# First tiles and first block issued from strings of single operations in a new order

## The chip, the cores and the metric

One core of a Trainium2 chip runs the kernel. TensorE (PE, with its weight loads PEld), VectorE (DVE), ScalarE (ACT) and GpSimd (POOL) each work through their own queue in order; SyncE (SP) issues the DMAs. The metric is the device time of one execution in microseconds; profiles give times from the start of their span.

## The reference

Attention within chunks of 64 tokens, then two matrix products with an ELU between. q, k and v are float32, the weights float64.

```python
scores = scale * np.matmul(q_c, k_c.transpose(0, 1, 2, 4, 3))   # 8 x 8 heads, 9 chunks of 64, head size 64
scores = scores - np.max(scores, axis=-1, keepdims=True)
attn = np.exp(scores)
attn = attn / (np.sum(attn, axis=-1, keepdims=True) + 1e-09)
out = np.matmul(attn, v_c)
...
h = x @ w_in                                                    # 4608 x 512 by 512 x 2048
g = np.where(h > 0.0, h, alpha * (np.exp(np.minimum(h, 0.0)) - 1.0))
return (g @ w_out).astype(np.float32)
```

## The kernel before

The 4608 tokens are nine blocks of 512, a block four tiles of 128 tokens; the hidden size of 2048 is sixteen tiles f of 128. Each operand of a product is held as a high and a low part (xhi, xlo; wi_hi, wi_lo; ghi, glo; wo_hi, wo_lo), and a product is three matmuls (`three`, L419): high by high, high by low, low by high. So the hidden product of one f (`hidden`, L428) is 4 x 3 matmuls into a bank h, and the second product of one f (`second_products`, L867, through a queue) 4 x 3 matmuls into the banks o of the four tiles. Between them stands `elu` (L436): relu and exp on ACT, one operation on DVE (e), ghi on ACT, glo on DVE. On PE the order is h0, h1, o0, h2, o1 and so on, one f apart.

The weights are 64-bit floats. They come in seventeen units: unit u holds the slice u of w_in (stored as `moe_w_in`) and the slice u - 1 of w_out. A unit takes two conversions on ACT (`prepare_units`, L128: "high" at L135, "low" at L140), three steps on DVE (L164, L171, L177), behind the third a copy of each high part on ACT (L184, wi_hi and wo_hi), and a subtraction of each low part on DVE (L155, wi_lo and wo_lo). Three staging buffers (`st`) take turns, and a unit's load is issued when the third step of the unit two earlier is done.

`early_attention` (L265) handles a tile in ten steps: transposes of q and k on PE (L271), their copies qT and kT on ACT (L278), scores (L249), maximum and subtraction on DVE (L284, L300), exponential on ACT (L304), sums and scaling on DVE (L306 to L309), turning on PE (L316), a copy on ACT (L323), the product with v (L257), and the splitting into xhi on ACT and xlo on DVE (L413, L414). Tiles named in `BY_HEAD` take eight exponentials of one head each, which also give the sums (L294), in place of one exponential and DVE's subtraction and sum.

The program has no scheduler for PE, ACT, DVE and SP: each engine's queue is the order in which the code is written. The first four tiles follow the string `START` (a digit advances that tile by a step, r is a conversion, d a DVE step or subtraction of a unit, w a number of transposes of the identity matrix). The first block follows `FIRST_BLOCK`, four lines that serve all four groups of four f alike: H is `hidden`, e a step of `elu`, a a step of the group's early tile (tiles 4 to 7, which belong to the second block), P the second products of the f before, X the splitting of the second block's x into xhi and xlo (`split_next`, L847). Ahead of H the program makes sure that the unit of that f is split (`split_upto`). `LOADS` gives the order of the first DMAs. Before h0 ten transposes of the identity are issued. POOL is scheduled by itself; its first work is at the end of the first block (`combine`, L476).

Of the kernel before, what the change touches and what calls it, by code (L numbers as in the profile page):

```python
# [10 lines left out]
F32 = mybir.dt.float32  # L11
# [9 lines left out]
def kernel(  # L21
# [19 lines left out]
    nc = tc.nc  # L41
# [104 lines left out]
    def split_units():  # L146
# [6 lines left out]
        def subtract(u: int):  # L153
            for (hi, lo), w in before:
                nc.vector.tensor_tensor(out=lo, in0=w, in1=hi.bitcast(F32), op=ALU.subtract)  # L155
                yield
            split.append(u)

        before = []
        for u in range(NU):  # L160
# [14 lines left out]
            if u > 2:  # L175
                yield from subtract(u - 1)
# [3 lines left out]
            if PRELOADED <= u + 2 < NU:  # L180
                load_unit(u + 2)
            before = [(part, y[:, i].bitcast(F32)) for i, part in enumerate(parts)]
            for (hi, _), w in before:
                nc.scalar.copy(out=hi, in_=w)  # L184
# [6 lines left out]
    split = []  # L191
    splitting = split_units()

    def split_upto(u: int):
        while u not in split:
            next(splitting)
# [68 lines left out]
    def early_attention(tt: int, q_sb, k_sb, v_sb, kT, at, a_pool, pool, put, by_head: bool):  # L265


        both = pool.tile([P, 2, DM], F32, name="ps_a")
# [57 lines left out]
        multiply_v(x_ps, v_sb, aT.rearrange("p h (u t) -> p u h t", u=2))  # L326
# [392 lines left out]
    def warm(n: int):  # L719

        warm_ps = ps_start.tile([P, 2, DM], F32, name="ps_a")[:, 0, :].rearrange(
            "p (i t) -> p i t", i=4)
        for i in range(n):
            nc.tensor.transpose(out=warm_ps[:, i % 4, :], in_=ident, identity=ident)  # L724
# [3 lines left out]
    LOADS = "q0 k0 q1 k1 q2 k2 u0 q3 k3 v0 v1 u1 v2 v3"  # L728
    BY_HEAD = (3,)
    START = (  # L730
        "w13 0 1 0 1 0 0 1 0 2 2 2 1 3 0 r 0 1 1 3 3 1 r 0 0 2 3 2 d 1 3 d d 2 r 3 1 2 d 3 d 2 0 "
        "3 2 1 2 3 w10 3 r d d d d r r d"
    )
    FIRST_BLOCK = (
# [64 lines left out]
    PRELOADED = sum(item[0] == "u" for item in LOADS.split())  # L799
# [10 lines left out]
    with (  # L810
# [4 lines left out]
        loaded = {}  # L815
        for item in LOADS.split():
            kind, n = item[0], int(item[1:])
            if kind == "u":
                load_unit(n)
            else:  # L820
                loaded[item] = load_heads(
                    {"q": q, "k": k, "v": v}[kind], f"{kind}_sb", n * P, start)
        tiles = [early_attention(
            tt, *[loaded[f"{kind}{tt}"] for kind in "qkv"],
            start.tile([P, NK, P], F32, name="kT"), start, start, ps_start, split_first_x,
            tt in BY_HEAD,
        ) for tt in range(NTT)]
        for item in START.split():
            if item[0] == "w":
                warm(int(item[1:]))  # L830
            else:
                next({"d": splitting, "r": preparation}.get(item) or tiles[int(item)])
# [5 lines left out]
    wi1 = plain.enter_context(tc.tile_pool(name="wi1", bufs=1))  # L838
    weights.append((*w_in_tiles(wi1), *later_w_out))
    io = plain.enter_context(tc.tile_pool(name="io", bufs=2))  # L840
    ps_h = ctx.enter_context(tc.tile_pool(name="ps_h", bufs=2, space=bass.MemoryType.PSUM))
    ps_o = ctx.enter_context(tc.tile_pool(name="ps_o", bufs=1, space=bass.MemoryType.PSUM))
    early = ctx.enter_context(ExitStack())
    ps_early = early.enter_context(
        tc.tile_pool(name="ps_early", bufs=1, space=bass.MemoryType.PSUM))
# [7 lines left out]
    def early_tile(n: int):  # L853

        n0 = n * P
        loaded = [load_heads(src, name, n0, pool)
                  for src, name, pool in ((q, "q_sb", io), (k, "k_sb", io), (v, "v_sb", vio))]
        return early_attention(
            n % NTT, *loaded, k_turned, at, wi1, ps_early, lambda tt, src: keep_x(tt, src), True)
# [14 lines left out]
    following = early_tile(NTT)  # L874
    for blk in range(PLAIN - 1):
        if blk == 1:
            early.close()
            ps_a = ctx.enter_context(
                tc.tile_pool(name="ps_a", bufs=1, space=bass.MemoryType.PSUM))
        run = blk * TB, o_tiles(), None  # L880
        for f in range(NF):
            tt, st = divmod(f, 4)
            n = (blk + 1) * NTT + tt + 1
            if st == 0:
# [160 lines left out]
```

## Time and profile before

| | us |
|---|---|
| median of 3 runs (845.35 to 848.22) | 846.59 |
| the profiled execution | 848.72 |
| its span | 846.7 |
| first matmul of h0 | 26.74 |
| first matmul of o0 | 38.47 |
| first matmul of the second block's first hidden product | 133.32 |

Rows of the timeline and of the chain of waits begin with start and duration in us, then engine, line of the kernel, operation and tiles; what stands in brackets is the idle time of that engine just before and what ended it. Rows of the windows give the stretch, its length, the busy time of each engine with the number of its instructions, the granted clock of TensorE as a share of full speed, the busy share of the DMA engines (over 1 where transfers overlap) and GB/s.

### The profile page before, as it was taken

What the parts mean: (1) busy time and instruction counts of PE and PEld (TensorE: products, weight loads), DVE (VectorE), ACT (ScalarE), POOL (GpSimd) and SP (SyncE); (2) the same over time, 40 slices, a digit from 0 to 9 for tenths busy, and PEclk for the clock granted to TensorE, in tenths of its full rate; (3) what the DMA queues carried; (4) which work ended last, traced back from release to release, by engine and by line L of the source; (5) the groups of instructions that cost most, each with busy time, mean ns of one, the idle gap of its engine ahead of it and who ended that gap; (6) DMA issues with size and microseconds to landing.
All of it is one profiled execution on the core that took longest, in us unless ns stands there. A gap on an engine that the chain in (4) does not pass through costs nothing.

```text
span 846.7 us, 15737 instructions
## 1 busy us (share of the span) xinstructions
PE 829.1 (98%) x5959; PEld 678.1 (80%) x5959; DVE 501.2 (59%) x717; ACT 483.7 (57%) x855; POOL 176.5 (21%) x148
## 2 busy tenths in 40 slices
PE   6899999999999999999999999999999999999998
PEld 5687887888878887888888888788888888888786
DVE  5888996666775769666666745666555333233411
ACT  6799985544564547656656436556664355555521
POOL 0000005355302120211113531111126211111120
PEclk9799999999999999999999999999999999999999
DMA  9877672767768786698887656798854365545231
GB/s 240 259 214 228 220 223 75 223 201 240 240 191 229 207 220 183 185 252 247 236 257 243 183 151 208 197 257 242 225 159 137 109 195 162 164 142 161 92 108 50
DMA packets 178795, 164.10 MB, mean 194 GB/s; under 512 B 65568, under 2 KB 161312, under 8 KB 178720
## 3 DMA queue, kind: packets, MB, share of 16 engines
q1 hardware_dynamic: 178720, 163.10, 66.0%
q8 instruction: 47, 0.77, 0.4%
q14 instruction: 28, 0.23, 0.1%
HBM read 131.07 MB, written 28.31 MB: 188 GB/s over the span
## 4 chain that ended last, share of the span: by engine, by line
PE 90%; ACT 3%; DMA 2%; DVE 2%; SPq 1%; issue 1%; DVEq 0%; ACTq 0%
PE o L422 44%; PE h L422 41%; PE ps_a L249 2%; PE ps_a L257 2%; SPq L213 1%; DMA k_sb<-in_k_dram 1%; PE ps_a L316 1%; DMA v_sb<-in_v_dram 1%; DMA wi_hi<-a_dram 1%; DMA turned<-unturned 0%; DVE g_kept L590 0%; PE ps_a L271 0%; ACT e L440 0%; ACT e L587 0%; DVE xlo L850 0%
## 5 line engine op out<-in xcount | busy, mean ns | idle before, releaser
L422 PE MATMUL o<-wo_hi,ghi 128*128 128x512 f32 x416 | 165.4, 398 | 0.0
L422 PE MATMUL o<-wo_hi,glo 128*128 128x512 f32 x416 | 163.1, 392 | 0.2 <-DMA wi_hi<-a_dram 0.2
L422 PE MATMUL o<-wo_lo,ghi 128*128 128x512 f32 x416 | 162.8, 391 | 0.0
L597 POOL TENSOR_TENSOR glo<-e,ghi 128x512 fp32r<-128x512 f32 x46 | 59.6, 1296 | 317.3 <-ACT ghi L595 311.8
L422 PE MATMUL h<-xhi,wi_hi 128*128 128x512 f32 x336 | 112.1, 392 | 0.1
L422 PE MATMUL h<-xlo,wi_hi 128*128 128x512 f32 x336 | 111.4, 390 | 0.7 <-DVE xlo L850 0.7
L422 PE MATMUL o<-wo_hi,wo_lo 128*128 128x512 f32 x320 | 99.8, 390 | 1.0 <-DVE kept L455 1.0
L422 PEld LDWEIGHTS o<-wo_hi,ghi 128*128 128x128 f32 x416 | 78.6, 189 | 17.4 <-ACT ghi L447 0.2
L422 PEld LDWEIGHTS o<-wo_hi,glo 128*128 128x128 f32 x416 | 78.5, 189 | 17.5 <-DVE glo L450 1.0
L422 PEld LDWEIGHTS o<-wo_lo,ghi 128*128 128x128 f32 x416 | 78.6, 189 | 15.8
L636 ACT COPY kept<-h 128x512 f32<-128x512 f32 x72 | 42.3, 588 | 61.6 <-PE h L422 61.6
L422 PE MATMUL h<-wi_lo,wi_hi 128*128 128x512 f32 x288 | 75.0, 396 | 0.0
L422 PE MATMUL h<-xhi,wi_lo 128*128 128x512 f32 x192 | 74.9, 390 | 0.0
L422 PEld LDWEIGHTS h<-xlo,wi_hi 128*128 128x128 f32 x336 | 63.1, 188 | 14.0 <-DVE xlo L850 1.1
L422 PEld LDWEIGHTS h<-xhi,wi_hi 128*128 128x128 f32 x336 | 63.1, 188 | 13.6 <-PE ps_a L724 0.3
L422 PE MATMUL h<-wo_lo,wi_hi 128*128 128x512 f32 x288 | 73.0, 389 | 0.0
L422 PEld LDWEIGHTS o<-wo_hi,wo_lo 128*128 128x128 f32 x320 | 60.1, 188 | 14.4 <-DVE kept L455 1.9
L590 DVE SCALAR_TENSOR_TENSOR g_kept<-e,g_kept 128x512 f32<-128x512 f32 x48 | 35.5, 739 | 57.7 <-ACT e L587 57.7
L640 DVE TENSOR_TENSOR g_kept<-h,kept 128x512 f32<-128x512 f32 x48 | 33.1, 689 | 51.7 <-ACT kept L636 27.2
L422 PEld LDWEIGHTS h<-wo_lo,wi_hi 128*128 128x128 f32 x288 | 54.1, 188 | 11.2
L587 ACT ACTIVATE e<-e 128x512 f32<-128x512 f32 x96 | 60.7, 633 | 3.1
L422 PE MATMUL o<-wo_lo 128*128 128x512 f32 x160 | 62.3, 389 | 0.0
(107 smaller groups left out, 1318.0 us busy)
## 6 DMA issues: line engine op xcount, KB each, us to landing
wi_hi<-a_dram SPq DMA_DIRECT2D x168, 256.0 KB, 3.9
wo_lo<-lo_dram SPq DMA_DIRECT2D x52, 512.0 KB, 4.7
kept<-in_q_dram SPq DMA_DIRECT2D x100, 128.0 KB, 3.4
kept<-in_k_dram SPq DMA_DIRECT2D x100, 128.0 KB, 3.8
st<-in_moe_w_in_dram SPq DMA_DIRECT2D x16, 512.0 KB, 4.9
v_sb<-in_v_dram SPq DMA_DIRECT2D x32, 256.0 KB, 5.8
st<-in_moe_w_out_dram SPq DMA_DIRECT2D x16, 512.0 KB, 5.3
a_dram<-kept SPq DMA_DIRECT2D x16, 512.0 KB, 4.0
```

The costliest lines, as they stand in the source:

```text
L213: nc.sync.dma_start(out=dst[p0:p0 + n], in_=src[b, :, s0:s0 + n, :].rearrange("h s d -> s h d"))
L249: nc.tensor.matmul(scores[halves[c], j, hp, :], lhsT=qT[halves[j], hp, halves[c]], rhs=kT[halves[j], hp, halves[c]], start=True, stop=True,)
L257: nc.tensor.matmul(x_ps[halves[j], c, hp, :], lhsT=v_sb[halves[c], 2 * hp + j, :], rhs=aT[halves[c], :, j * NK + hp], start=True, stop=True,)
L316: nc.tensor.matmul(turned_ps[half, h, :], lhsT=a[half, h, :], rhs=ident[half, half], start=True, stop=True,)
L422: nc.tensor.matmul(ps, lhsT=a, rhs=b, start=start, stop=stop, skip_group_check=onto)
L587: nc.scalar.activation(out=e, in_=e, func=AF.Exp, scale=-1.0)
L590: nc.vector.scalar_tensor_tensor(out=to, in0=e, scalar=-1.0, in1=c, op0=ALU.add, op1=ALU.max)
L597: engine.tensor_tensor(out=lo, in0=e, in1=hi.bitcast(F32), op=ALU.subtract)
L636: nc.scalar.copy(out=c21 if i == 4 else self.kept[i - 1], in_=x_ps)
L640: nc.vector.tensor_tensor(out=to, in0=y_ps, in1=self.kept[kept], op=ALU.add)
```

## The change

`LOADS` goes; the loads stand in `START` now, with q, k and v of the four tiles ahead of unit 0, and unit 2 among them. `FIRST_BLOCK` becomes one string of single operations for all sixteen f: besides H, e, P, X a digit advances that tile, L begins a tile's loads, u loads a unit, r is a conversion, d a DVE step of a unit, s one subtraction of a low part (now apart from the steps, `subtract_next`), l writes a low part of w_out to memory, K begins the loads for tile 8. `split_upto` goes, and the order of the strings alone holds. The ten transposes before h0 go. `hidden` of f = 0, in each of the three blocks that use it, takes the eight matmuls with xhi first and the four with xlo last. Tile 2 in place of tile 3, and tiles 4 and 5 but not 6 and 7, are handled by head (before, tiles 4 to 7 all were). Pools whose memory was used by the first tiles wait for single tiles of it (`reuse_waits`). Behind X a copy of one element on POOL reads the last xlo and writes where one of POOL's additions writes later.

```diff
-        def subtract(u: int):
-            for (hi, lo), w in before:
-                nc.vector.tensor_tensor(out=lo, in0=w, in1=hi.bitcast(F32), op=ALU.subtract)
-                yield
-            split.append(u)
-
-        before = []
...
-            if u > 2:
-                yield from subtract(u - 1)
             nc.vector.scalar_tensor_tensor(
                 out=y, in0=high, scalar=0x80000000, in1=y, op0=ALU.bitwise_and, op1=ALU.bitwise_or
             )
-            if PRELOADED <= u + 2 < NU:
-                load_unit(u + 2)
-            before = [(part, y[:, i].bitcast(F32)) for i, part in enumerate(parts)]
-            for (hi, _), w in before:
-                nc.scalar.copy(out=hi, in_=w)
-            yield
-            if u <= 1:
-                yield from subtract(u)
-        yield from subtract(NU - 1)
+            for i, (hi, _) in enumerate(parts):
+                nc.scalar.copy(out=hi, in_=y[:, i].bitcast(F32))
+                merged.append((parts[i], y[:, i].bitcast(F32)))
+            yield
+
+    def subtract_next():
+        (hi, lo), w = merged.pop(0)
+        nc.vector.tensor_tensor(out=lo, in0=w, in1=hi.bitcast(F32), op=ALU.subtract)
...
-    def early_attention(tt: int, q_sb, k_sb, v_sb, kT, at, a_pool, pool, put, by_head: bool):
-
-
-        both = pool.tile([P, 2, DM], F32, name="ps_a")
+    def early_attention(tt: int, q_sb, k_sb, get_v, kT, at, a_pool, get_banks, put, by_head: bool):
+
+
+        both = get_banks()
...
-        multiply_v(x_ps, v_sb, aT.rearrange("p h (u t) -> p u h t", u=2))
+        multiply_v(x_ps, get_v(), aT.rearrange("p h (u t) -> p u h t", u=2))
...
-        for kt in range(NK):
-            three(h, hi[:, kt, :], lo[:, kt, :], xhi[:, kt, :], xlo[:, kt, :],
-                  kt == 0, kt == NK - 1)
+        if f:
+            for kt in range(NK):
+                three(h, hi[:, kt, :], lo[:, kt, :], xhi[:, kt, :], xlo[:, kt, :],
+                      kt == 0, kt == NK - 1)
+        else:
+            terms = [(w, xhi, kt) for w in (hi, lo) for kt in range(NK)]
+            terms += [(hi, xlo, kt) for kt in range(NK)]
+            for i, (w, x, kt) in enumerate(terms):
+                nc.tensor.matmul(h, lhsT=w[:, kt, :], rhs=x[:, kt, :], start=i == 0,
+                                 stop=i == len(terms) - 1)
...
-    LOADS = "q0 k0 q1 k1 q2 k2 u0 q3 k3 v0 v1 u1 v2 v3"
-    BY_HEAD = (3,)
+    BY_HEAD = (2, 4, 5)
...
-        "w13 0 1 0 1 0 0 1 0 2 2 2 1 3 0 r 0 1 1 3 3 1 r 0 0 2 3 2 d 1 3 d d 2 r 3 1 2 d 3 d 2 0 "
...
+        "q0 k0 q1 k1 w13 v0 0 1 0 q2 0 k2 q3 0 k3 1 1 v1 0 2 v2 1 3 0 2 2 v3 1 2 3 u0 3 1 2 u1 0 "
+        "r r 1 3 1 0 3 2 2 d u2 d 1 0 r d 3 3 2 s 2 0 r d 1 d 3 r 2 3 3"
...
-        "r H e d e a r e a d d e P",
...
+        "H r u3 r d L4 d e s 4 d 4 e e s r d e u4 H d s 4 e s r P e 4 d e e H 4 e d 4 L5 e s u5 d "
...
+        def start_step(item: str):
+            tt = int(item)
+            if tt not in tiles:
+                tiles[tt] = early_attention(
+                    tt, *[loaded[kind, tt] for kind in "qk"], lambda: loaded["v", tt],
+                    start.tile([P, NK, P], F32, name="kT"), start, start,
+                    lambda: start_banks() if tt else warmed[0],
+                    split_first_x, tt in BY_HEAD)
+            next(tiles[tt])
...
+            elif kind == "r":
+                next(preparation)
+            elif kind == "d":
+                next(merging)
+            elif kind == "s":
+                subtract_next()
...
-    wo1 = ctx.enter_context(tc.tile_pool(name="wo1", bufs=1))
+                start_step(item)
+
+    wo1 = ctx.enter_context(tc.tile_pool(name="wo1", bufs=1, reuse_waits="tile"))
     later_w_out = w_out_tiles(wo1)
-    gp = ctx.enter_context(tc.tile_pool(name="gp", bufs=2))
+    gp = ctx.enter_context(tc.tile_pool(name="gp", bufs=2, reuse_waits="tile"))
...
+    ps_h = ctx.enter_context(tc.tile_pool(name="ps_h", bufs=2, reuse_waits="tile", space=bass.MemoryType.PSUM))
+    ps_o = ctx.enter_context(tc.tile_pool(name="ps_o", bufs=1, reuse_waits="tile", space=bass.MemoryType.PSUM))
...
+            n % NTT, q_sb, k_sb, lambda: v_sb, k_turned, at, wi1,
+            lambda: ps_early.tile([P, 2, DM], F32, name="ps_a"),
+            lambda tt, src: keep_x(tt, src), n in BY_HEAD)
...
+    run, f, early_tiles = (0, o_tiles(), None), -1, {}
+    for item in FIRST_BLOCK.split():
+        if item == "H":
+            f += 1
+            act, acted = elu(hidden(f)), 0
+        elif item == "e":
+            g, acted = next(act), acted + 1
+            if acted == 4:
+                second(f, *g)
+        elif item == "P":
+            second_products()
+        elif item[0] == "L":
+            early_tiles[item[1]] = early_tile(int(item[1]))
+        elif item in early_tiles:
...
+        elif item == "X":
+            split_next()
+            nc.gpsimd.tensor_copy(out=kept_st[1][:, :1], in_=xlo[:, NK - 1, :1].bitcast(F32))
+
+    early.close()
+    ps_a = ctx.enter_context(tc.tile_pool(name="ps_a", bufs=1, space=bass.MemoryType.PSUM))
```

Three places in the queues. The first is SP's queue at its start: the loads of the four tiles (q_sb, k_sb, v_sb) and of the weight units (st). Before:

```order
L213 DMA q_sb<-in_q_dram 128x8x64
L213 DMA k_sb<-in_k_dram 128x8x64
L114 DMA st<-in_moe_w_in_dram 128x4x256
L213 DMA q_sb<-in_q_dram 128x8x64
L213 DMA k_sb<-in_k_dram 128x8x64
L213 DMA v_sb<-in_v_dram 128x8x64 x2
L114 DMA st<-in_moe_w_in_dram 128x4x256
L121 DMA st<-in_moe_w_out_dram 128x1024
L213 DMA v_sb<-in_v_dram 128x8x64 x2
```

Now, behind q, k of tiles 0 and 1:

```order
L199 DMA v_sb<-in_v_dram 128x8x64
L199 DMA q_sb<-in_q_dram 128x8x64
L199 DMA k_sb<-in_k_dram 128x8x64
L199 DMA q_sb<-in_q_dram 128x8x64
L199 DMA k_sb<-in_k_dram 128x8x64
L199 DMA v_sb<-in_v_dram 128x8x64 x3
L114 DMA st<-in_moe_w_in_dram 128x4x256 x2
L121 DMA st<-in_moe_w_out_dram 128x1024
```

The first weights stood between tiles 2 and 3 and are now behind all twelve loads of the tiles; v of tile 0 is fifth.

The second is ACT's queue from the last xhi to the first tile of the first block (lines of the changed kernel differ: L432 and L433 are relu and exp of h0, L440 is ghi, L264 the copies of tile 4). Before:

```order
L413 CAST xhi<-ps_a 128x2x4x64 x3
L140 ACTIVATE st<-st 128x1024
L184 CAST wi_hi<-xf 128x4x128
L184 CAST wo_hi<-xf 128x512
L135 ACTIVATE st<-st 128x1024
L140 ACTIVATE st<-st 128x1024
L135 ACTIVATE st<-st 128x1024
L439 ACTIVATE e<-h 128x512
L440 ACTIVATE e<-e 128x512
L140 ACTIVATE st<-st 128x1024
L447 CAST ghi<-e 128x512
L278 COPY qT<-ps_a 128x512
```

Now:

```order
L399 CAST xhi<-ps_a 128x2x4x64 x2
L140 ACTIVATE st<-st 128x1024
L135 ACTIVATE st<-st 128x1024
L172 CAST wi_hi<-xf 128x4x128
L172 CAST wo_hi<-xf 128x512
L432 ACTIVATE e<-h 128x512
L433 ACTIVATE e<-e 128x512
L264 COPY qT<-ps_a 128x512
L264 COPY k_turned<-ps_a 128x512
L440 CAST ghi<-e 128x512
L140 ACTIVATE st<-st 128x1024
```

Two of the five wide conversions are gone from ahead of ghi (they stand among the xhi copies now), one is behind it, and tile 4's copies are ahead of it.

The third is PE's queue into h0 and h1. Before:

```order
L316 MATMUL ps_a<-ident,a 64x64 x32
L257 MATMUL ps_a<-qT,v_sb 64x64 x32
L724 MATMUL ps_a<-ident 128x128 x10
L422 MATMUL h<-xhi,wi_hi 128x512
L422 MATMUL h<-xlo,wi_hi 128x512
L422 MATMUL h<-xhi,wi_lo 128x512
```

Now:

```order
L302 MATMUL ps_a<-ident,a 64x64 x16
L243 MATMUL ps_a<-qT,v_sb 64x64 x32
L425 MATMUL h<-xhi,wi_hi 128x512 x4
L425 MATMUL h<-xhi,wi_lo 128x512 x4
L425 MATMUL h<-xlo,wi_hi 128x512 x4
L257 MATMUL ps_a<-ident,q_sb 128x128 x4
```

The transposes of the identity are gone, and the matmuls that read xlo stand at the end of h0. At the block's end the order on PE was h15, v's product of tile 7, o14, first hidden product of the second block, o15; it is now h14, h15, o13, o14, first hidden product of the second block, o15, with the last step of tile 7 ahead of o12.

More of the change, by code (lines that the diff above doesn't have):

```diff
@@ L798 @@
     )
-    PRELOADED = sum(item[0] == "u" for item in LOADS.split())
     ctx.enter_context(tc.manual_schedule(engines={
@@ L814 @@
         make_identity(nc, ident)
[L815 to L819, printed above, removed]
-            else:
[L821 to L832, printed above, removed]
-    wo1 = ctx.enter_context(tc.tile_pool(name="wo1", bufs=1))
+        loaded, tiles, warmed = {}, {}, []
+        def start_banks():
+            return ps_start.tile([P, 2, DM], F32, name="ps_a")
+        def start_step(item: str):
[7 more added lines that the diff above has]
+            next(tiles[tt])
```

149 lines of the change are left out of this document (70 added, 79 removed), and 9 rows, old and new, of the table FIRST_BLOCK.

## The prediction, on record before the changed kernel ran

> **What bounds the kernel now.** First the page: TensorE (PE) is busy for 98% of the span, so a gain can only come from where it is idle or slow.
>
> ```profile
> PE 829.1 (98%) x5959; PEld 678.1 (80%) x5959; DVE 501.2 (59%) x717; ACT 483.7 (57%) x855; POOL 176.5 (21%) x148
> PEclk9799999999999999999999999999999999999999
> ```
>
> 846.7 - 829.1 = 17.6 us of PE idle time, and one slice of forty with a lower clock, the second (21 to 42 us). The windows (busy time of PE, PEld, DVE, ACT, POOL, then clock, DMA share, GB/s) place both.
>
> ```profile
> 10.00:13.00 3.00, 1.76 (x41) 1.18 (x38) 2.86 (x7) 2.57 (x5) 0.00 (x0) 1.00 1.07 249
> 18.00:22.00 4.00, 1.65 (x57) 1.41 (x51) 3.79 (x10) 3.58 (x16) 0.00 (x0) 1.00 1.11 312
> 22.00:26.00 4.00, 4.00 (x100) 3.82 (x96) 2.86 (x6) 3.19 (x7) 0.00 (x0) 0.57 1.05 378
> 20.00:60.00 40.00, 35.35 (x347) 29.04 (x348) 34.45 (x49) 34.12 (x64) 0.00 (x0) 0.87 0.78 233
> 33.40:37.40 4.00, 0.04 (x1) 0.00 (x1) 3.05 (x5) 3.97 (x8) 0.00 (x0) 0.80 0.83 262
> 35.90:42.60 6.70, 5.20 (x42) 4.21 (x43) 6.67 (x10) 5.64 (x21) 0.00 (x0) 0.50 0.63 223
> 60.00:120.00 60.00, 60.00 (x468) 48.44 (x467) 54.14 (x77) 54.00 (x115) 0.00 (x0) 1.00 0.74 231
> ```
>
> From 60 to 120 us PE has no gap: there the first block is bound by PE, with DVE and ACT 90% busy behind it. What can be won lies ahead of 43 us and at the block's end. I call the hidden product of hidden tile f hf (12 matmuls), the second product of f of (12), and those of the next block h0', h1'. The timeline shows the joints: last xhi copy, first matmul of h0, last of h1, the scores of tile 4, first of o0.
>
> ```profile
> 25.28 0.59 ACT L413 CAST xhi<-ps_a 128x512 fp32r<-128x512 f32 x1 [0.27 <-PE ps_a L257]
> 26.74 0.47 PE L422 MATMUL h<-xhi,wi_hi 128*128 128x512 f32 x1
> 33.05 0.39 PE L422 MATMUL h<-xhi,wi_lo 128*128 128x512 f32 x1
> 37.40 1.14 PE L249 MATMUL ps_a<-k_turned,qT 64*64 64x64 f32 x32 [3.97 <-ACT k_turned L278]
> 38.47 0.79 PE L422 MATMUL o<-wo_hi,ghi 128*128 128x512 f32 x1
> ```
>
> PE stands still for 4 us ahead of o0, waiting for ACT, and then finds its clock halved (0.50 from 35.9 to 42.6 us). The chain of waits prices that: o0 took 4.88 us, a later o 2.95, an undisturbed h 2.7; and from h2 to h15 one round takes (127.18 - 43.41)/13 = 6.44 us.
>
> ```profile
> 38.54 4.88 PE o L422 x12
> 43.41 2.74 PE h L422 x12
> 47.23 2.95 PE o L422 x12
> 127.18 2.73 PE h L422 x12
> ```
>
> **Term 1: the wait ahead of o0.** Here is ACT's queue over it.
>
> ```profile
> 29.47 0.62 ACT L184 CAST wi_hi<-xf 128x512 fp32r<-128x512 f32 x1 [2.55 <-DVE xf L177]
> 30.52 1.14 ACT L135 ACTIVATE st<-st 128x1024 f32<-128x1024 f32 x1
> 31.56 1.13 ACT L140 ACTIVATE st<-st 128x1024 uint32<-128x1024 uint16 x1
> 32.60 1.13 ACT L135 ACTIVATE st<-st 128x1024 f32<-128x1024 f32 x1
> 33.63 0.58 ACT L439 ACTIVATE e<-h 128x512 f32<-128x512 f32 x1
> 34.77 1.11 ACT L140 ACTIVATE st<-st 128x1024 uint32<-128x1024 uint16 x1
> 36.77 0.58 ACT L278 COPY k_turned<-ps_a 128x512 f32<-128x512 f32 x1
> ```
>
> ACT idles 2.55 us for unit 1, then does four wide conversions (1.04 from start to start) among which h0's relu and tile 4's copies wait their turn. The changed order does unit 1's second conversion and unit 2's first already among the xhi copies, puts unit 3's second behind ghi, and lets tile 4's copies go ahead of ghi. I follow the new queues with these rows.
>
> ```profile
> 2.00:8.00 6.00, 5.42 (x60) 4.78 (x58) 0.00 (x0) 1.49 (x4) 0.00 (x0) 1.00 1.12 253
> 6.91 0.66 PE L271 MATMUL ps_a<-ident,k_sb 128*128 128x128 f32 x4 [0.29 <-DMA k_sb<-in_k_dram]
> 7.49 0.69 PE L249 MATMUL ps_a<-kT,qT 64*64 64x64 f32 x32
> 8.33 0.69 DVE L284 TENSOR_REDUCE mx<-ps_a 128x8 f32<-128x512 f32 x1 [8.33 <-PE ps_a L249]
> 10.48 0.59 ACT L278 COPY qT<-ps_a 128x512 f32<-128x512 f32 x1
> 10.96 0.59 ACT L278 COPY kT<-ps_a 128x512 f32<-128x512 f32 x1
> 17.38 0.32 ACT L294 ACTIVATE a<-ps_a,mx 128x64 f32<-128x64 f32 x1
> 19.71 0.66 ACT L184 CAST wi_hi<-xf 128x512 fp32r<-128x512 f32 x1
> ```
>
> Loads: q, k, v move at 253 GB/s from 2.0 us, and the fourth load (1.05 MB, by bytes at 6.1 us) was awaited until 6.9, so one lands 0.8 behind its bytes. Tile 3's k is now ninth (2.36 MB): 2.0 + 9.3 + 0.8 = 12.1. Its transposes (0.66), tile 2's scores (0.69, behind them on PE), the maximum (0.69), 14.2, and 0.4 for its small scaling and the handovers bring ACT to tile 2's eight exponentials at 14.6. From there ACT's queue is full up to the last xhi: eight exponentials 2.3 (17.38 to 19.71), unit 0 two at 0.6, six copies (four aT, xhi0, xhi1) at 0.5 (10.48 to 10.96), one exponential 0.6, three wide conversions 1.04, wi_hi 0.55, xhi2 and xhi3 1.1: 2.3 + 1.2 + 3.0 + 0.6 + 3.1 + 0.55 + 1.1 = 11.9, so 26.5. All twelve q, k, v are in by bytes at 14.4, units 0 and 1 (1.57 MB at 378 GB/s) at 18.6, landed by 19.4 to 20.4; ACT wants unit 1 at 19.8. With half a microsecond there (20.3) and 0.2 for tile 3's product, **h0 starts at 27.2, not before 26.74**: the last xhi comes later, but two wide conversions more are done. The reordered h0 needs xlo only in its ninth matmul, 1.8 us on, and DVE ends xlo at 28.0. The ten dropped transposes filled time in which PE waited anyway: nothing.
>
> On from there: four ACT pieces (two wide, two casts: 3.1) end at 30.3, h0 at 30.1; relu and exp to 31.5, tile 4's two copies to 32.5, ghi to 33.1. PE: transposes to 31.4, h1 to 34.1, scores to 34.9. DVE from 28.0 does five narrow operations up to glo's end, 0.7 each with the handovers, and three wide ones of 1.15 (by the rows below narrow ones are 0.69 long and stand 0.60 apart; wide ones are 1.23 long, so some 1.15 apart): 34.9.
>
> ```profile
> 28.21 1.23 DVE L177 SCALAR_TENSOR_TENSOR xf<-st,xf 128x1024 uint32<-128x1024 uint32 x1
> 30.13 0.69 DVE L155 TENSOR_TENSOR wi_lo<-xf,wi_hi 128x512 fp32r<-128x512 f32 x1 [0.69 <-ACT wi_hi L184]
> 30.73 0.69 DVE L155 TENSOR_TENSOR wo_lo<-xf,wo_hi 128x512 fp32r<-128x512 f32 x1
> ```
>
> PE and DVE both come to o0 at 34.9: 38.47 - 34.9 = **-3.6 us**.
>
> **Term 2: the slow o0.** Without the 4 us of idling the clock doesn't fall there: 2.95 - 4.88 = **-1.9**.
>
> **Term 3: the block's end.** h0' began, waited for DVE's xlo, and o15 followed at 137.09.
>
> ```profile
> 133.32 0.40 PE L422 MATMUL h<-xhi,wi_hi 128*128 128x512 f32 x1
> 133.72 2.48 DVE L850 TENSOR_TENSOR xlo<-xf,xhi 128x512 fp32r<-128x512 f32 x4
> 134.45 0.50 PE L422 MATMUL h<-xlo,wi_hi 128*128 128x512 f32 x1 [0.73 <-DVE xlo L850]
> 137.09 0.39 PE L422 MATMUL o<-wo_hi,ghi 128*128 128x512 f32 x1
> ```
>
> 3.77 us in place of 2.72. In the new order o13 and o14 both lie between h15 and h0' (5.4 us), in which relu, exp, four xhi and four xlo fit, and xlo is wanted last: **-1.05**. The one-element copy on POOL and the narrower waits on reused memory issue nothing that PE waits for: 0. The third block's h0 is reordered too, but waited for nothing: 0.
>
> **Term 4: clock at h0.** Before h0 the new queue gives PE little: from 21.3 to 27.2 us tile 3's turns and the products of tiles 2 and 3, three groups of 32 small matmuls at 0.69 (the 7.49 row), 2.1 of 5.9 us, with gaps of up to 1.4. The windows speak both ways: 59% busy from 10 to 13 us left the clock at 1.00, 41% from 18 to 22 was followed by 0.57 from 22 to 26; the share is nearer to the second, but no gap is as long as that ahead of o0. Ends: nothing, or h0's 2.7 once more at half the clock. The rows don't decide; I take half, **+1.3**.
>
> [...]
>
> **Term 5: new waits in rounds 1 to 5.** Much preparation is moved early here. From xlo's end to glo of f = 5 the new DVE queue holds 30 narrow operations at 0.6, 13 wide ones at 1.15 and two tiles' maxima and scalings, some 1.95 each (two of 0.69, three small ones taken at 0.2): 18 + 15 + 3.9 = 36.9 us. PE asks for it at 34.9 + 5 x 6.44 = 67.1, 39.1 us after 28.0: 94% of DVE. From 60 to 120 us DVE showed 90%; at that rate it needs 41.0, 1.9 late. Ends 0 and 1.9; **+1.0**. Later rounds ask for less. Tiles 6 and 7 by one exponential take 1.7 off ACT each and give DVE 1.2 each, where slack has grown: 0, and 2.4 if that slack is gone.
>
> Sum: -3.6 - 1.9 - 1.05 + 1.3 + 1.0 = **-4.25**. The profiled execution took 848.72 us (span 846.7, 2.0 around it), 2.1 above the median of 846.59; nothing in it looks disturbed, so I take the difference off the median: **842.3**.
>
> **Rivals.** *The clock stays up* (0.2): no gap is long enough; 1.3 less gives 841.0, and 840.0 without new waits too. [...] *DVE becomes the bound* (0.2): at the 86% of 20 to 60 us (34.45/40) it needs 42.9 for 39.1, 3.8 late in place of 1.0: 845.1. For it: 94% is more than any long stretch shows; against: its idle time was partly lack of work. *Slower through unit 1's landing* (0.1): in the new queue its conversion stands ahead of wi_hi and every xhi, and each microsecond beyond the 20.3 taken moves h0 by one. From 4.25 later, 24.6, the change loses; with a landing at 27 it takes 849. Against: 4.7 MB are in by 18.6 at the rates shown. *The early start doesn't happen* (0.05): h0 waits for all of xlo after all, as any reader of its banks, and ACT's backlog ahead of k_turned remains: terms 1 and 2 fall away, 846.6 less term 3 and with no new waits, 845.5. The forecast itself has 0.45, with 840.5 to 844.
>
> **Numbers.** Faster by over 0.3% (2.5 us, about what a measurement here can tell from no change) means below 844.05: forecast, clock and a third of the DVE case: 0.72. Same, up to 849.1: 0.2. Slower: 0.08, most of the late landing. The range leaves out a tenth on each side: from 839.3 (clock up, no waits, unit 1 early) to 846.5.
>
> **What would show it.** First h at 27.2 with clock near 1 or 0.5; no wait of PE's scores for k_turned, first o near 35 to 37; twelve o's in 2.95; PE's waits for glo or wi_lo on DVE under 2 us up to 70 us; h0' without a wait for xlo. An h0 past 30 us, or PE waiting anew in rounds 6 to 14, would make it wrong.

## The result and the profile after

The changed kernel took 843.53 us (median of seven runs, 841.12 to 844.01) and the kernel before, on the same chip, 848.57 (seven runs, 845.35 to 849.93): a ratio of 0.994 with an interval of 0.9921 to 0.9958. The profiled execution has a span of 841.8 us, 4.9 under that of before.

First the page: busy time by engine, and the granted clock in forty slices.

```profile
PE 824.9 (98%) x5949; PEld 673.8 (80%) x5949; DVE 504.1 (60%) x719; ACT 480.2 (57%) x825; POOL 176.7 (21%) x149
PEclk9999999999999999999999999999999999999999
```

TensorE's idle time is 841.8 - 824.9 = 16.9 us, hardly less than the 17.6 of before; what it lost is 4.2 us of *busy* time (the ten dropped transposes are part of it), and the dent in the second slice of the clock is gone. A matmul at half the clock counts as busy for longer (in the kernel before, o0 took 4.88 us, with the clock at 0.50 from 36 to 42 us, and a later o 2.95 at 1.00), so the share of busy time (98% both times) shows nothing of it. Next the windows of the changed kernel, with the same columns as before.

```profile
22.00:26.00 4.00, 1.63 (x67) 1.53 (x67) 3.52 (x8) 4.00 (x8) 0.00 (x0) 1.00 0.88 278
20.00:60.00 40.00, 35.88 (x419) 29.12 (x415) 37.85 (x55) 37.58 (x71) 0.00 (x0) 1.00 0.81 241
60.00:120.00 60.00, 60.00 (x523) 48.05 (x522) 57.06 (x81) 52.82 (x93) 1.66 (x2) 1.00 0.69 219
```

Ahead of h0 PE has less to do than it had (1.63 of 4 us from 22 to 26, where it had been 4.00 at 0.57), which costs nothing by itself. DVE and ACT work 37.85 and 37.58 of the 40 us from 20 to 60, where it had been 34.45 and 34.12: preparation is done earlier. The joints, from the timeline (start, duration, engine, line, operation, tiles, idle time before):

```profile
15.54 0.31 ACT L280 ACTIVATE a<-ps_a,mx 128x64 f32<-128x64 f32 x1 [0.65 <-DVE mx L276]
21.30 1.14 ACT L135 ACTIVATE st<-st 128x1024 f32<-128x1024 f32 x1 [0.70 <-DMA st<-in_moe_w_out_dram]
26.87 1.08 ACT L399 CAST xhi<-ps_a 128x512 fp32r<-128x512 f32 x2
28.00 1.20 PE L425 MATMUL h<-xhi,wi_hi 128*128 128x512 f32 x4 [1.33 <-ACT xhi L399]
33.46 0.59 ACT L264 COPY k_turned<-ps_a 128x512 f32<-128x512 f32 x1
34.68 0.69 PE L235 MATMUL ps_a<-k_turned,qT 64*64 64x64 f32 x32
35.31 0.50 PE L408 MATMUL o<-wo_hi,ghi 128*128 128x512 f32 x1
35.52 0.68 DVE L443 TENSOR_TENSOR glo<-e,ghi 128x512 fp32r<-128x512 f32 x1
36.26 0.50 PE L408 MATMUL o<-wo_hi,glo 128*128 128x512 f32 x1 [0.22 <-DVE glo L443]
```

h0 starts later than before, at 28.00 (26.74), but o0 earlier, at 35.31 (38.47): 7.31 us lie between them in place of 11.73, and the scores of tile 4 wait for nothing. Last the chain of waits (start, duration, product): h2 and o15 of the changed kernel, and o15 of the kernel before; then the block's end from the timeline.

```profile
38.83 2.72 PE h L408 x12
131.59 2.72 PE o L408 x12
137.25 2.72 PE o L422 x12
```

```profile
127.36 2.49 DVE L858 TENSOR_TENSOR xlo<-xf,xhi 128x512 fp32r<-128x512 f32 x4
128.71 1.07 PE L425 MATMUL h<-xhi,wi_hi 128*128 128x512 f32 x4
130.52 1.07 PE L425 MATMUL h<-xlo,wi_hi 128*128 128x512 f32 x4
131.43 0.39 PE L408 MATMUL o<-wo_hi,ghi 128*128 128x512 f32 x1
```

h2 begins 4.58 us earlier than before (38.83 for 43.41, both by the chain). At the block's end xlo is done at 129.85, h0' wants it at 130.52 and waits for nothing; o15 begins at 131.43 in place of 137.09, 5.66 earlier (by the chain, which puts it 0.16 later in both, 131.59 and 137.25). From there on the two programs have the same products to do, and the changed one took 0.8 us longer for them in its profile (841.8 - 131.43 = 710.4; 846.7 - 137.09 = 709.6). Over all profiles of this study the way from o15 to the end, by the chain, is between 708.0 and 710.8 us, with no tie to any edit: below, small differences are read at o15 (by the chain, where the changed kernel has 131.59), and the whole time only where more than about 2 us are at stake. The start scatters as well. Among the profiles that share the order of the changed kernel up to h0 (the two of that kernel, runs 1, 2 and 8), h0 came between 27.99 and 28.91, so a difference at o15 counts only beyond that, or when it is taken from h0 on.

### The profile page after: what moved, and what is told of

Its sections match the earlier page's. It is cut to its first block, busy times and chain, and to the rows that moved or that the text cites. A ratio compares the mean times of both kernels' runs of the same rounds, so it can differ in the third digit from the quotient of the medians.

```text
span 841.8 us, 15683 instructions
## 1 busy us (share of the span) xinstructions
PE 824.9 (98%) x5949; PEld 673.8 (80%) x5949; DVE 504.1 (60%) x719; ACT 480.2 (57%) x825; POOL 176.7 (21%) x149
## 4 chain that ended last, share of the span: by engine, by line
PE 85%; DVE 5%; DMA 3%; SPq 2%; ACT 2%; issue 1%; DVEq 0%; ACTq 0%
PE o L408 42%; PE h L408 38%; PE ps_a L235 2%; SPq L199 2%; PE ps_a L243 2%; DMA v_sb<-in_v_dram 1%; DMA kept<-in_k_dram 1%; DMA k_sb<-in_k_dram 1%; DMA st<-in_moe_w_out_dram 1%; DMA turned<-unturned 1%; PE ps_a L302 1%; DVE xf L573 0%; ACT e L433 0%; DVE e L435 0%; DVE g_kept L583 0%
## 5 line engine op out<-in xcount | busy, mean ns | idle before, releaser
L408 PE MATMUL h<-xhi,wi_hi 128*128 128x512 f32 x324 | 108.1, 394 | 0.0
L408 PE MATMUL h<-xlo,wi_hi 128*128 128x512 f32 x324 | 106.7, 389 | 0.0
L408 PEld LDWEIGHTS h<-xhi,wi_hi 128*128 128x128 f32 x324 | 60.8, 188 | 12.9
L408 PEld LDWEIGHTS h<-xlo,wi_hi 128*128 128x128 f32 x324 | 60.9, 188 | 12.3
L408 PE MATMUL h<-xhi,wi_lo 128*128 128x512 f32 x180 | 70.2, 390 | 0.0
```

The source lines that it names most:

```text
L408: nc.tensor.matmul(ps, lhsT=a, rhs=b, start=start, stop=stop, skip_group_check=onto)
```

## Experiments

All start from the changed kernel unless said. The kernel before was run beside each group and had medians of 848.13 (runs 1 to 4), 847.65 (runs 5 to 8), 848.83 (runs 9 and 10) and 848.31 (run 11).

**1. h0 in the old order.** `hidden` of f = 0 mixes xhi and xlo again, in all three blocks.

```diff
-        if f:
+        if True:
```

> The changed kernel with the twelve matmuls of the first hidden product (f = 0, all three blocks) in the old interleaved order. Theory: at the start h0's second matmul then waits for the last xlo (ends at 28.8 in the changed kernel, where h0 begins at 28.0), so h0 ends 0.6 later and o0 follows it by about as much; at the block's end nothing changes, because o13 and o14 lie between h15 and h0' and xlo's first slices are there before h0' begins. Sum 0.5 to 0.8 us slower than the changed kernel. Rival: the new order of f = 0 is what removed the wait at the block's end; then h0' waits again by 0.7 to 1.1 us, the sum is 1.3 to 1.9 us.

Measured: 843.75 us, ratio 0.995 (0.9933 to 0.9968). PE's timeline at h0, and the window behind it:

```profile
28.79 0.50 PE L408 MATMUL h<-xhi,wi_hi 128*128 128x512 f32 x1 [1.32 <-ACT xhi L399]
29.63 0.50 PE L408 MATMUL h<-xlo,wi_hi 128*128 128x512 f32 x1 [0.33 <-DVE xlo L400]
33.85 0.60 PE L257 MATMUL ps_a<-ident,q_sb 128*128 128x128 f32 x4
```

```profile
30.00:34.00 4.00, 4.00 (x13) 3.09 (x12) 3.14 (x4) 1.89 (x3) 0.00 (x0) 0.57 0.73 202
```

The second matmul waits 0.33 us for xlo, and in this execution the clock fell at h0, so that it took 33.85 - 28.79 = 5.06 us with that wait; o15 is at 133.96. At the block's end h0' waited for nothing in this order too (2.72 us by the chain). So the order inside `hidden` is not what removed the wait for xlo at the block's end, and it costs little at h0 but for the clock (the median is 0.2 to 0.9 us over the two of the changed kernel, 843.53 and, in run 5, 842.88).

**2. o13 back between h14 and h15.** The place of o13 and o14 is the other candidate for the block's end.

```diff
-        "e P s e e H d e e s e e d l11 H P e e d K l12 P s X e l13 e"
+        "e P s e e H d e e s P e e d l11 H e e d K l12 P s X e l13 e"
```

> The changed kernel with one group of second products put back ahead of h15 (h14, o13, h15, o14, h0'). Theory: the place of the second products is what covers the splitting of the next x. In the changed kernel the four xhi end 5.4 us and the four xlo 6.4 us after h15's end; with 2.7 us of cover in place of 5.4, h0' waits for xhi by about 2 us in all: 1.5 to 2.5 us slower than the changed kernel. Rival: the order within h0' is the cover, the place of the products hardly matters: under 0.5 us.

Measured: 846.17 us (ten runs), ratio 0.9986 (0.9976 to 0.9995): 2.6 to 3.3 us over the two medians of the changed kernel, more than expected, and more than half the gain gone by one token. PE's timeline at h0', and the window:

```profile
130.49 2.21 PE L425 MATMUL h<-xhi,wi_hi 128*128 128x512 f32 x4 [1.13 <-ACT xhi L857]
132.50 1.91 PE L425 MATMUL h<-xhi,wi_lo 128*128 128x512 f32 x4
134.20 1.76 PE L425 MATMUL h<-xlo,wi_hi 128*128 128x512 f32 x4
```

```profile
132.00:136.00 4.00, 3.98 (x11) 3.16 (x11) 3.61 (x5) 0.52 (x2) 2.73 (x4) 0.57 1.02 223
```

With one product less for cover, h0' waits 1.13 us for xhi (the changed kernel: nothing), its first four matmuls come at the pace of the copies (2.21 for 1.07; ACT's four xhi take 2.18), and then the clock halves for the rest (0.50 from 133 to 135 us; 1.91 and 1.76 for 1.07). o13 is the cover. The wait and the pacing, 1.13 + 1.14 us, have the size expected; the halved clock behind them adds 0.84 + 0.69 in this profile.

**3. The kernel before, with h1 computed twice.** The repeated twelve matmuls fill PE's idle time ahead of o0; nothing else changes. It tells term 2 (the clock) apart from term 1 (the wait).

```diff
-        for kt in range(NK):
-            three(h, hi[:, kt, :], lo[:, kt, :], xhi[:, kt, :], xlo[:, kt, :],
-                  kt == 0, kt == NK - 1)
+        doubled = f == 1 and not once
+        if doubled:
+            once.append(f)
+        for _ in range(2 if doubled else 1):
+            for kt in range(NK):
+                three(h, hi[:, kt, :], lo[:, kt, :], xhi[:, kt, :], xlo[:, kt, :],
+                      kt == 0, kt == NK - 1)
...
+    once = []
```

> The kernel before with h1 of the first block computed twice into the same bank, 2.7 us of needless PE work in the gap of 4 us ahead of o0. Theory: the idle gap drops the clock; filled to 1.4 us, o0 begins at the same time (it waits for k_turned) and takes 2.95 in place of 4.8 us, and the scores ahead of it 0.7 in place of 1.1: 2.0 to 2.4 us faster than the kernel before, although PE does more. Rival: o0's slowness is something else (operands, ACT and DVE behind): no gain, 0 to 1 us slower because relu of h1 comes later.

Measured: 847.84 us (ten runs), ratio 1.0 (0.9991 to 1.001) against before. PE's timeline:

```profile
27.69 0.47 PE L422 MATMUL h<-xhi,wi_hi 128*128 128x512 f32 x1 [0.16 <-DVE xlo L414]
38.40 0.69 PE L249 MATMUL ps_a<-k_turned,qT 64*64 64x64 f32 x32 [1.28 <-ACT k_turned L278]
39.02 0.50 PE L422 MATMUL o<-wo_hi,ghi 128*128 128x512 f32 x1
41.87 0.39 PE L422 MATMUL h<-xhi,wi_hi 128*128 128x512 f32 x1
```

The wait shrank from 3.97 to 1.28 us, and o0 took 41.87 - 39.02 = 2.85 us in place of 4.78 (38.47 to 43.25): the half clock in o0 goes with the long idle time ahead of it (from 38 to 42 us it is 1.00 here, 0.50 before), at a price of some 2 us. The whole time did not show the 2.0 to 2.4 us expected. From h0 to o15 the profile is 1.65 us shorter than that of before (27.69 to 136.55, in place of 26.74 to 137.25). But in it h0 started 0.95 us later than in that of before, and behind o0 PE lost some more, 0.59 of 4 us, as a window shows:

```profile
42.00:46.00 4.00, 3.41 (x35) 2.63 (x35) 3.65 (x8) 4.00 (x17) 0.00 (x0) 1.00 0.28 67
```

That explains one execution, not a median of ten. For the sum this run decides nothing; for the cause of the slow o0 it speaks, with one profile, for the clock.

**4. Unit 2's first conversion back behind the last xhi.** One of the two conversions that were moved ahead on ACT.

```diff
-        "... s 2 0 r d 1 d 3 r 2 3 3"
+        "... s 2 0 r d 1 d 3 2 3 3"
...
-        "H r u3 r d L4 ..."
+        "H r r u3 r d L4 ..."
```

> The changed kernel with unit 2's first conversion on ACT (1.04 us) moved back behind the last xhi, where it stood before. Theory: ACT's queue from tile 2's exponentials to o0 is full, so what moves within it moves h0 but not o0: h0 begins 1.0 us earlier (27.0), relu of h0 is not earlier, o0 within 0.3 us, the whole within 0.5 us of the changed kernel. Rival: an earlier h0 carries through to o0 and the end: 0.8 to 1.0 us faster.

Measured: 841.85 us (four runs), ratio 0.9932 (0.9917 to 0.9947); o0 at 35.72, o15 at 132.00. In the profile o0 comes no earlier than in the changed kernel (35.31 and 35.18), as the theory had it; but h0 came at 28.22 and not at 27.0, since the start was late, with tile 2's exponentials at 16.34 (15.54). The median says otherwise: it is 1.0 to 1.7 us under the two of the changed kernel, where the rival had it (0.8 to 1.0 faster), and outside the 0.5 us that the theory allowed. The intervals of the ratios overlap (0.9921 to 0.9958 for the changed kernel), and the stretch behind o15 was the shortest of all here (708.0 us). So this run does not decide whether the place of one conversion matters.

**5. The changed kernel again,** with the three that follow, on another chip.

> The changed kernel once more, as the measure for the others of this group, and as a test of the clock. [...] Rival: the clock follows from the order alone and is 1.00 again in every window from 20 to 60 us.

Measured: 842.88 us (six runs), ratio 0.9947 (0.9932 to 0.9962); o15 is at 130.98. PE's timeline at the joints:

```profile
27.99 1.19 PE L425 MATMUL h<-xhi,wi_hi 128*128 128x512 f32 x4 [1.32 <-ACT xhi L399]
30.85 0.60 PE L257 MATMUL ps_a<-ident,q_sb 128*128 128x128 f32 x4
35.18 0.50 PE L408 MATMUL o<-wo_hi,ghi 128*128 128x512 f32 x1
```

The joints lie within 0.2 us of the first profile's, and h0 takes 30.85 - 27.99 = 2.86 us. But the clock took another course, as two windows show:

```profile
20.00:22.00 2.00, 2.00 (x58) 2.00 (x58) 1.97 (x3) 1.71 (x3) 0.00 (x0) 0.50 1.08 402
22.00:24.00 2.00, 1.91 (x73) 1.80 (x68) 1.73 (x6) 2.00 (x5) 0.00 (x0) 0.77 0.80 251
```

It fell at 20 us, where it was 1.00 in the first profile of the same program, and cost nothing that shows: h0 waited 1.32 us for ACT's xhi, in the first profile 1.33.

**6. The first weights early, as before,** with all other queues as changed.

```diff
-        "q0 k0 q1 k1 w13 v0 0 1 0 q2 0 k2 q3 0 k3 1 1 v1 0 2 v2 1 3 0 2 2 v3 1 2 3 u0 3 1 2 u1 0 "
+        "q0 k0 q1 k1 w13 q2 k2 u0 q3 k3 v0 v1 u1 v2 v3 0 1 0 0 0 1 1 0 2 1 3 0 2 2 1 2 3 3 1 2 0 "
```

> The changed kernel with the first loads in the order of before (unit 0 behind tile 2's k, unit 1 behind v of tile 1, v of tiles 2 and 3 last); all other queues as changed. Theory: the load order as such brings little. Tile 3's k lands 1 us later (tenth place in bytes), which moves tile 2's exponentials by 0.8 to 1.0; unit 1 lands earlier, and ACT's wait of 0.7 us for it goes. h0 and o0 move by -0.2 to +0.5 us, the whole by as much. Rival: q, k, v ahead of the units is what gives the gain; then 2 us or more are lost.

Measured: 843.03 us (four runs), ratio 0.9938 (0.9915 to 0.996). h0 came at 29.64, 1.65 us later than in run 5, and o15 1.67 later (132.65); PE's waits name the load that was passed (us in total, number, longest):

```profile
PE ps_a L257 <- DMA q_sb<-in_q_dram: 2.2, 1, 2.2
```

1.7 us at o15 would be more than expected. But the scatter of the start is as large. Here tile 2's exponentials began at 17.93; with the new order of the loads they began at 14.60 in run 11 and at 17.46 in run 10, whose last xhi came at 28.52 like that of this run. The medians are level (843.03 and 842.88). So no worth of the new order of the loads is shown, and the medians speak against the 2 us of the rival.

**7. All q and k first, v later,** which brings tile 3's k from the ninth place to the eighth and tile 2's from the seventh to the sixth.

```diff
-        "q0 k0 q1 k1 w13 v0 0 1 0 q2 0 k2 q3 0 k3 1 1 v1 0 2 v2 1 3 0 2 2 v3 1 2 3 u0 3 1 2 u1 0 "
+        "q0 k0 q1 k1 w13 q2 k2 q3 k3 v0 v1 u0 u1 v2 v3 0 1 0 0 0 1 1 0 2 1 3 0 2 2 1 2 3 3 1 2 0 "
```

> The changed kernel with q and k of all four tiles first, then v of tiles 0 and 1, units 0 and 1, then v of tiles 2 and 3; all other queues as changed. Theory: the chain to o0 starts with tile 3's k (now eighth, 1.0 us earlier; DVE waited 1.7 us for tile 2's scores) and runs through ACT, which waited 0.7 us for unit 1 (now 0.5 MB earlier). h0 and o0 come 1.0 to 1.7 us earlier, the whole is 0.8 to 1.7 us faster than the changed kernel. Rival: o0 is set by DVE or by unit 3's landing (ACT waited 0.7 us for it) and stays within 0.3 us.

Measured: 842.25 us (six runs), ratio 0.9939 (0.9922 to 0.9955). ACT's timeline and its waits:

```profile
14.14 0.31 ACT L280 ACTIVATE a<-ps_a,mx 128x64 f32<-128x64 f32 x1 [0.69 <-DVE mx L276]
27.11 1.06 ACT L399 CAST xhi<-ps_a 128x512 fp32r<-128x512 f32 x2
```

```profile
ACT st L135 <- DMA st<-in_moe_w_out_dram: 3.0, 3, 1.4
```

Tile 2's exponentials began 1.4 us earlier than in the changed kernel (14.14 for 15.54), and the last xhi 0.24 later (27.11 for 26.87): most of the lead went into waits for weight units, 3.0 us in three, where the changed kernel has 1.4 in two. Whether the lead itself comes from the order is open (run 11 had 14.60 with the order of the changed kernel). The start stands between two supplies, tile 3's k and the units. The theory was wrong in taking the first alone; h0 came at 28.22, o15 at 132.13, neither of them earlier, and the median is 0.6 to 1.3 us under those of the changed kernel, which is within their scatter.

**8. Tiles 6 and 7 by head again.**

```diff
-    BY_HEAD = (2, 4, 5)
+    BY_HEAD = (2, 4, 5, 6, 7)
```

> The changed kernel with tiles 6 and 7 by head as before (each 1.7 us more on ACT, 1.2 us less on DVE). Theory: from 60 us on PE waits for neither (DVE 97% busy, ACT 86% from 80 to 120 us, PE without a gap), so the whole stays within 0.3 us. Rival: DVE at 97% is the hidden bound and its relief makes it 0.5 us faster, or ACT falls behind and it is 1 us slower or more.

Measured: 843.14 us (four runs), ratio 0.9946 (0.9928 to 0.9964). From the start of h2 to that of o15 it took 92.82 us by the chain (39.13 to 131.95), in run 5 92.76 (38.22 to 130.98). Nothing, as predicted.

**9. ACT's wide conversions in their old places.** Two conversions return behind the last xhi, unit 3's second one ahead of ghi, tile 4's copies behind ghi.

```diff
-        "... s 2 0 r d 1 d 3 r 2 3 3"
+        "... s 2 0 1 3 2 3 3"
...
-        "H r u3 r d L4 d e s 4 d 4 e e s r d e u4 H d s 4 ..."
+        "H r d d r r u3 r d L4 d e s 4 d r e e s 4 d e u4 H d s 4 ..."
```

> ACT's queue from the last xhi to tile 4's copies stands as in the kernel before (unit 1's second and unit 2's first conversion behind the last xhi, unit 3's second ahead of ghi, tile 4's copies behind ghi); all else as changed. Theory (term 1 is this order of the queue): h0 starts up to 2 us earlier, at 26 to 27.5, and o0 comes some 11.7 us behind it as before, at 37.5 to 39, with PE waiting for k_turned or ghi for 2.5 us or more, and perhaps half the clock in o0; o15 is 2.5 to 4.5 later than in the changed kernel (130.98 and 131.59), the time 845.5 to 848. Rival (the start's loads and the new h0 bring o0 forward, the order on ACT does not, as moving one conversion alone showed): o0 at 35 to 36.3, time 842 to 844.

Measured: 843.7 us (six runs), ratio 0.9943 (0.9932 to 0.9955). PE's timeline:

```profile
27.54 1.19 PE L425 MATMUL h<-xhi,wi_hi 128*128 128x512 f32 x4 [0.70 <-ACT xhi L399]
36.42 0.69 PE L235 MATMUL ps_a<-k_turned,qT 64*64 64x64 f32 x32 [0.89 <-ACT k_turned L264]
37.05 0.50 PE L408 MATMUL o<-wo_hi,ghi 128*128 128x512 f32 x1
```

9.51 us from h0 to o0, between the 7.31 of the changed kernel and the 11.73 of before; o15 1.3 to 1.9 later than in the two profiles of the changed kernel (132.86). The time is the rival's, o0 neither side's (37.5 to 39 and 35 to 36.3). The queue was not quite the old one: unit 1's high copies (wi_hi, wo_hi) stood behind the conversions here, and ahead of unit 2's in the kernel before.

**10. The narrower waits on reused memory taken out** (`reuse_waits` of the seven pools made behind the first tiles). One line of the seven:

```diff
-    ps_h = ctx.enter_context(tc.tile_pool(name="ps_h", bufs=2, reuse_waits="tile", space=bass.MemoryType.PSUM))
+    ps_h = ctx.enter_context(tc.tile_pool(name="ps_h", bufs=2, space=bass.MemoryType.PSUM))
```

> The seven pools made behind the first tiles wait without reuse_waits, so h0's first matmul waits for DVE's last xlo; all else as changed. The prediction's price (nothing that PE waits for is issued): h0 at 28.0, as with it, 842 to 844. Rival (the narrower wait is what lets the reordered h0 begin ahead of xlo): h0 starts when xlo ends, 28.8 to 29, with the wait named for DVE, and 0.8 of it reaches o0 and o15; 0.5 to 1 us slower than the changed kernel, 843 to 845 (too near to tell by the median, to be read at the joints).

Measured: 845.77 us (six runs), ratio 0.9961 (0.9946 to 0.9975), 2.2 to 2.9 us over the changed kernel. The last xhi on ACT, the last xlo on DVE, and PE; then the window:

```profile
28.52 1.12 ACT L399 CAST xhi<-ps_a 128x512 fp32r<-128x512 f32 x2
```

```profile
29.18 1.29 DVE L400 TENSOR_TENSOR xlo<-ps_a,xhi 128x512 fp32r<-128x512 f32 x2 [0.21 <-ACT xhi L399]
```

```profile
30.52 1.64 PE L425 MATMUL h<-xhi,wi_hi 128*128 128x512 f32 x4 [2.17 <-DVE xlo L400]
34.97 0.60 PE L257 MATMUL ps_a<-ident,q_sb 128*128 128x128 f32 x4
```

```profile
30.00:34.00 4.00, 3.48 (x9) 2.79 (x10) 3.93 (x5) 2.77 (x4) 0.00 (x0) 0.63 0.56 139
```

xhi is there at 29.64, and h0 begins at 30.52, when DVE has read the last of the banks (30.47), though its first eight matmuls need no xlo. That is 0.9 us; and in this profile the clock fell, so that h0 took 34.97 - 30.52 = 4.45 us, where run 5 needed 2.86. (The start was also 1.7 us later by its last xhi.) The rival's mechanism holds, and the median lost more than its 0.5 to 1 us. That the longer idle time brings the drop of the clock about is not shown: run 1 had such a drop behind 1.32 us.

**11. ACT's queue as before, the high copies included,** and DVE's steps of units 1 to 3 in their old order.

```diff
-        "... s 2 0 r d 1 d 3 r 2 3 3"
+        "... s 2 0 d 1 3 2 3 3"
...
-        "H r u3 r d L4 d e s 4 d 4 e e s r d e u4 H d s 4 ..."
+        "H r d d s s r d r d u3 r L4 e 4 r e e 4 d d e u4 H s 4 ..."
```

> As the run with ACT's old queue, but with unit 1's two high copies too where they stood before, ahead of unit 2's conversions (the run before had left them behind), and DVE's steps of units 1 to 3 in their old order. Theory (term 1 is the order of the units' work around h0, and the 2.55 us in which ACT waited for DVE's third step of unit 1 are part of it): ACT idles 2 to 2.6 us ahead of wi_hi, o0 comes 11 to 12 us behind h0 as before (11.73), where the changed kernel had 7.3 and the run before 9.5; with h0 at 26.5 to 28 that is 37.5 to 40, PE idles 3 us or more ahead of it, perhaps with half the clock behind; time 846 to 849. Rival (the new loads bring unit 1 early enough, and the casts' place costs nothing more): o0 9.5 behind h0 as in the run before, 843 to 845.

Measured: 848.77 us (twelve runs), ratio 1.0007 (0.9992 to 1.0022): the whole gain is gone. ACT's timeline behind the last xhi, PE's at o0, and the window:

```profile
27.30 1.15 ACT L140 ACTIVATE st<-st 128x1024 uint32<-128x1024 uint16 x1
30.99 0.62 ACT L172 CAST wi_hi<-xf 128x512 fp32r<-128x512 f32 x1 [2.55 <-DVE xf L168]
32.04 1.14 ACT L135 ACTIVATE st<-st 128x1024 f32<-128x1024 f32 x1
```

```profile
27.45 1.19 PE L425 MATMUL h<-xhi,wi_hi 128*128 128x512 f32 x4 [0.70 <-ACT xhi L399]
38.97 0.69 PE L235 MATMUL ps_a<-k_turned,qT 64*64 64x64 f32 x32 [4.01 <-ACT k_turned L264]
39.59 0.79 PE L408 MATMUL o<-wo_hi,ghi 128*128 128x512 f32 x1
```

```profile
38.00:42.00 4.00, 3.03 (x38) 2.48 (x39) 3.61 (x7) 3.97 (x7) 0.00 (x0) 0.70 0.69 226
```

Everything of the old profile is back: ACT's 2.55 us of idling for unit 1, PE's 4.01 us for k_turned (3.97 before), 12.14 us from h0 to o0 (11.73), an o0 at a lowered clock (0.70 from 38 to 42 us; 4.54 us by the chain; 4.88), and o15 at 136.98. And this with the new loads, the new h0, the narrower waits and the new block's end in place. Against run 9, whose steps on DVE also stand in another order, the main difference is what follows unit 1's second conversion: there conversions of unit 2 ran while DVE made its steps for unit 1, here ACT stood still for them.

## Why the prediction held, and where its terms were off

The forecast of 842.3 (839.3 to 846.5) met 843.53, by its main path: the wait ahead of o0, the slow o0 and the wait at the block's end went, and they make up the gain. That the figure came so near is partly luck, as the last paragraph but one of this section shows. Term by term, in the profiled execution:

- **Term 1, the wait ahead of o0** (forecast -3.6): 38.47 to 35.31, -3.2. The mechanism is shown: run 11 puts the wait of 4 us back by the order on ACT and DVE alone, and run 9 tells its two parts apart. Letting ACT convert unit 2 while DVE works on unit 1, in place of waiting for it, is worth 2.5 us at o0 (39.59 to 37.05, h0 nearly alike) and 4.1 at o15 with the clock. The places of the conversions and of tile 4's copies are worth another 2.2 between h0 and o0 (9.51 to 7.31), but these conversions delay h0, and at o15 1.3 to 1.9 are left in single profiles, 0.2 to 0.8 in the medians. The size was off at h0, which came at 28.00 and not 27.2; o0 was only 0.4 late (35.31 for 34.9), since the way between them was 7.31 and not 7.7. The chain's first link gave tile 2's exponentials at 14.6, measured 15.54, and unit 1 was taken at 20.3, measured 21.30. Run 7 suggests that the first error alone did not matter, since the units would have been waited for.
- **The narrower waits** (forecast 0, in one sentence with the copy on POOL): wrong. That they issue nothing is true, but the forecast of h0 at the last xhi rested on them; without them it waits for xlo (run 10), 0.9 us and, in that profile, 1.6 more by the clock. Their benefit was in term 1 unnamed, so the sum was not harmed. The rival "the early start doesn't happen" had its mechanism right; in the changed kernel these waits kept it away.
- **Term 2, the slow o0** (forecast -1.9): h2 came 4.58 us earlier by the chain, of which 3.16 are term 1; the other 1.4 are o0's. The clock was full (1.00 from 34 to 42 us), as forecast, and in runs 3 and 11 the slow o0 went and came with the long wait ahead of it (1.28 us and an o0 of 2.85; 4.01 and 4.54). The forecast had glo, DVE's last piece, ready at 34.9 with PE; it came at 36.20, and o0's third matmul waited 0.22 us for it. ACT had stood 0.73 us for unit 3's load, and DVE 0.92 us for wi_hi behind it, waits that the forecast did not have. In run 5, without them, o0 took 2.87 us (35.18 to 38.05), and the 1.9 came in full (4.78 - 2.87).
- **Term 3, the block's end** (forecast -1.05): 92.76 us from h2 to o15 by the chain (131.59 - 38.83) for 93.84 (137.25 - 43.41): -1.08. The cover is o13 (run 2), not xlo's place at the end of h0' (run 1).
- **Term 4, the clock at h0** (forecast +1.3, half of two ends): 0 in the profile, whose clock stayed at 1.00. It did fall there in run 1 and in run 10 (0.57 and 0.63 from 30 to 34 us), with a loss of 1.9 us (5.06 - 0.33 - 2.86) and 1.6 in h0, so the upper end of 2.7 was too high. The rival "the clock stays up" is what happened here, in both profiles of the changed kernel; its reason, that no gap is long enough, was an estimate that the runs do not bear out, since in run 2 the clock fell behind a wait of 1.13 us. Half of two ends is a size that no single execution takes. Nor does one program always take the same course: run 5 had a drop at 20 us (0.50 from 20 to 22) which the first profile of the same program has not (1.00), with joints within 0.2 us.
- **Term 5, DVE's waits in rounds 1 to 5** (forecast +1.0): none behind that one for glo. From 60 to 120 us DVE was 57.06 / 60 = 95% busy, and PE had no gap. The step that failed is the rate: DVE's 90% of before was taken as what it can do, when part of it was want of work, as the rival itself had said against it.
- **Tiles 6 and 7** (0): run 8 agrees.

At o15 the sum of the terms was to be -4.25 and was -5.66: terms 4 and 5 took off 2.3 that did not come, and terms 1 and 2 promised 0.9 too much (5.5 for 4.58). That these errors went against each other is luck. 0.8 us of the difference came back behind o15 in that profile, where the programs are alike and runs scatter over 2.8 us. In absolute terms the forecast came out 1.2 too low though the gain was larger than forecast: the difference was taken off a median of three, 846.59, and further runs gave 847.65 to 848.83 for the kernel before. The profiled execution's own 848.72 was the typical one.

What stays open: the median of run 3 did not move though its o0 was 2 us shorter, and that of run 4 fell though its joints did not; no run here settles either. The ten dropped transposes and the one-element copy on POOL (both forecast at nothing) and tile 2 by head in place of tile 3 were never undone, so what they are worth is not shown. Nor were the terms undone one by one against each other: taken away alone, o13's place, the narrower waits and the order on ACT cost about 3, 2.5 and 5 us, more together than the whole gain, so they cannot be added up.

## What to carry to other kernels

Where an engine's queue waits for a neighbour that is working on the same item (here ACT for DVE's steps of unit 1), put independent pieces between: undoing that order on ACT and DVE took the whole gain of this change away (run 11, ratio 1.0007). Look for PE time not only in its gaps but in what runs behind them, since in runs 1, 2 and 10 a wait of 1.13 to 2.17 us was followed by a loss of 1.5 to 1.9 us at a lowered clock (0.57, 0.57 and 0.63 over 4 us). And an edit that only narrows a wait has the worth of every start that assumes it (h0 began 0.9 us behind the last xhi without it in run 10): name it in the sum.

## What the runs showed of the hardware

The clock halved with only short idle times ahead: 1.13 us of waiting with four paced matmuls behind it (run 2, 0.50 from 133 to 135 us), 2.17 us (run 10, 0.50 from 32 to 34), and in run 1 1.32 us ahead of h0 (0.54 from 30 to 32), where the changed kernel had 1.33 and kept 1.00. Neither the last wait nor the share of work decides alone: from 22 to 26 us the changed kernel had PE busy for 1.63 of 4 us and stayed at 1.00, where 1.65 of 4 from 18 to 22 in the kernel before were followed by 0.57. What does decide is not shown.

With one and the same order of loads, tile 2's exponentials began between 14.60 us (run 11) and 17.46 (run 10), with 15.5 in both profiles of the changed kernel. PE's waits for q_sb and k_sb up to 18 us came to 1.2 us in run 11 and 2.7 in run 10: about half of the difference stands with these first loads. The rows, from ACT's timeline, run 11 first:

```profile
14.60 0.31 ACT L280 ACTIVATE a<-ps_a,mx 128x64 f32<-128x64 f32 x1 [0.65 <-DVE mx L276]
17.46 0.31 ACT L280 ACTIVATE a<-ps_a,mx 128x64 f32<-128x64 f32 x1 [1.08 <-DVE mx L276]
```
